# A gated mix of a diagonal SSM and an FFN on one core: three of B's seven slots are turned by DMA instead of TensorE, and the gates and C's scalings move in the order

## The chip, the cores and the metric

One core of a Trainium2 chip. The metric is device time in microseconds of one execution; the kernel before has a median of 138.81 us in 3 runs (138.67 to 138.88). The engines named are TensorE (PE, matrix products; PEld is its weight load), VectorE (DVE), ScalarE (ACT), GpSimd (POOL) and SyncE (SP), which here issues most of the DMAs. Each engine works through its own instructions in order; semaphores join them.

## The reference

For x of 2048 tokens by 448 features in bf16:

```python
g = sigmoid((x * gate_w).sum(-1, keepdims=True))
Lam_bar = exp(dt * Lam);  B_bar = ((Lam_bar - 1) / Lam)[:, None] * Bmat      # complex, 448 states
h[t] = Lam_bar * h[t-1] + B_bar @ x[t]
a = 2 * real(h @ Cmat.T) + x * Dskip
b = silu(x @ w1) @ w2                                                        # w1 448x1792, w2 1792x448
out = g * a + (1 - g) * b
```

## The kernel before, in words

**Stretches and slots.** The tokens are cut into four stretches of 512 (`tc` 0 to 3). The 448 complex states lie in seven slots of 128 partitions: slots 0 to 2 are the real parts of states 0 to 383, slots 4 to 6 their imaginary parts, and slot 3 holds the last 64 states, real parts in the lower half and imaginary parts in the upper. The recurrence is made real by turning each state by its own angle (tables `COS` and `SIN`), so that what is left is a decaying scan with one real factor per state.

**Work on TensorE, which is written out by hand.** For a stretch, `F(tc)` is fourteen tiles of silu(x w1), each 128 columns of w1 by 512 tokens, and `B(tc)` seven tiles of Bu, one for each slot. `x_products` takes tiles in pairs that share two PSUM banks; a pair is 14 matmuls of 64 rows, 8 in its first half and 6 in its second, and the first half of the next pair stands before the second half of the last one. `G` (line 837) is the second FFN product for 128 tokens, `C` (line 858) the readout for 128 tokens. The order is F(0) tiles 0 to 7 (`NHF`), B(0), the rest of F(0), B(1), F(1) with most of B(2), G for tokens of stretches 0 and 1, the rest of B(2) within F(2), B(3), F(3), C for stretches 0 and 1, G and C for stretch 2, G and C for stretch 3.

**Around it.** A product needs B with the feature on the partitions, so B must be transposed. Two ways exist: `rows_B` loads rows into `Bnat` (which lies in UG2), `b_transposes` (lines 666 to 676) turns them with 64x64 transposes on TensorE, and DVE and ACT copy the result from PSUM into `BT`; or `turn_B` issues a transposing DMA (line 452) straight into `BT`. Before, the real parts and slot 3 (slots 0 to 3) take the first way in two groups of two slots (`BPE`), 16 transposes a group, and the imaginary parts (slots 4 to 6) the second. `evict` takes pairs out of PSUM: silu on ACT for F (line 696), DVE for B of stretch 0 (703), ACT for later B (705). `lanes(tc)` is the recurrence of a stretch on DVE: products with the tables (767), seven scans (799), products back (767), with POOL casting each scan to bf16 by DMA (417), ACT doing this for the last stretch (809). `gates(tc)` computes g and x Dskip times g: two DVE products `xg` and `xd` (767) and eleven ACT steps (899 to 906). `readout_weights` scales C: two ACT copies (884, 885) and two DVE operations (887) for each of four slots of `ct`. `ffn2` ends in a DMA on POOL that adds into xnat (845). The readout is evicted by DVE (868) except for token blocks 8 to 11 (ACT, 863).

**Who sets the order of the other engines.** A planner (`Plan.order`) places every operation of ACT, DVE, POOL and SP in time from a cost of each, a priority (`prio`, lower goes first) and an earliest time (`at`), and what comes out is the fixed order of each engine. `GPR` are the priorities of the gates of the four stretches, `CTAT` is the earliest planned time of C's ACT copies, `LORD` the order of the loads on SP after the first ones, and `W1CUTS` the columns at which w1's load is cut. `MB`, `MP`, `GAT` say where parts of B(2) and the gates stand.

Of the kernel before, what the change touches and what calls it, by code (L numbers as in the profile page):

```python
# [28 lines left out]
XT1 = "da"  # L29
XDMA = (1, 2, 3)  # L30
XAFT = ["PO1"]
LORD = "Br BI w1 x1 g n1 w2 x2 C n2 n3".split()
BPE = ((0,2),(2,4))
TRATE = 2
MERGE = True
NHF = 8
MB = 6
MP = 3
GAT = 10
W1CUTS = [0, 256, 512, 1024, 1792]  # L40
L2AT = 1
UDVE = (0, 1, 2, 3, 4, 5, 6)
OUTA = (8, 9, 10, 11)
PRMF = (1, 0)
PRMP = 9.7
CPP = 20.5
CTAT = 59.0
GPR = (14, 20.3, 21.5, 19)
CASTB = (360000, 360000, 360000)
XCOL = [0, 128, 256, 320]  # L50

# [254 lines left out]
def bass_gated_mix__ssm_conv_s5__dense_activation_silu__prompt_kernel(nc, A_x, A_Lambda_re, A_Lambda_im, A_B_re, A_B_im, A_C_re, A_C_im,  # L306
               A_log_dt, A_Dskip, B_x, B_w1, B_w2, gate_w, out):
    with ExitStack() as ctx:
# [66 lines left out]
        g = sb("g", [128, NTB], F32)  # L375
# [5 lines left out]
        def sem():  # L381
            _s[0] += 1
            return E(nc.semaphore(name=f"d{_s[0]}"))
# [30 lines left out]
        def load(q, dst, src, name, nbytes, prio=None, after=()):  # L414
            nl[0] += 1
            prio = nl[0] if prio is None else prio
            P.add(q, lambda e: e.dma_start(dst, src), list(after), name.split(), 0.6 if q == "pool" else 0.5 if nbytes > 2000 else 0.35, prio, sem(), nbytes, tag="ld " + name)  # L417

        w1cuts = W1CUTS

# [21 lines left out]
        Bnat = UG[2][:, :, 0:D_MOD]  # L442
# [22 lines left out]
        def turn_B(a, r0, r1, to, slots):  # L465

            for c, n in ((0, 3), (3, 1)):
                names = [f"BT{s}T{c}_{to}" for s in slots]
                for s, m in zip(slots, names):
                    btn[s] = (btn[s] if s == 3 or c else []) + [m]  # L470
                turn(BT[:, c:c + n, to:to + r1 - r0], a[r0:r1, XCOL[c]:XCOL[c] + 128 * n], " ".join(names), (r1 - r0) * 256 * n, 0.7 + 0.0042 * n * (r1 - r0) / 4 * 1.0)

        def rows_B(a, r0, s0, s1, p0):
            if s1 - s0 > 1:
                load("sp", Bnat[:, s0:s1, :], a[r0:r0 + 128 * (s1 - s0), :].rearrange("(b p) d -> p b d", p=128), " ".join(f"U2_{s}" for s in range(s0, s1)), 128 * (s1 - s0) * 896)
            else:
                load("sp", Bnat[p0:p0 + 64, s0, :], a[r0:r0 + 64, :], f"U2_{s0}" + "i" * (p0 == 64), 64 * 896)

        def rows_g():
# [7 lines left out]
            "w4": lambda: [load_w1("sp", 4, r, r + 2) for r in (0, 2)],  # L487
            "Br": lambda: (rows_B(A_B_re, 0, 0, 3, 0), rows_B(A_B_re, 384, 3, 4, 0), rows_B(A_B_im, 384, 3, 4, 64)),
            "Bi": lambda: rows_B(A_B_im, 0, 4, 7, 0),
            "B2": lambda: rows_B(A_B_re, 0, 0, 2, 0),  # L490
            "BR": lambda: turn_B(A_B_re, 0, 448, 0, (0, 1, 2, 3)),
            "BH": lambda: turn_B(A_B_re, 256, 448, 256, (2, 3)),
# [6 lines left out]
        }  # L499
        for k in LORD:  # L500
            do[k]()
# [208 lines left out]
        def x_products(tiles, fill={}, wait=()):  # L710

            part = (list(zip([(i, 64) for i in (0, 1, 2, 3)], [(i, 0) for i in (0, 1, 3, 2)])),
                    list(zip([(i, 0) for i in (0, 1, 2)], [(i, 64) for i in (0, 1, 3)])))
            pairs = [tiles[t:t + 2] for t in range(0, len(tiles), 2)]
            toks = [Ps(2) for _ in pairs]

            def steps(k, h, a, z):
                def body(pe):
                    for n, cut in list(enumerate(part[h]))[a:z]:
                        for b, ((i, p0), tile) in enumerate(zip(cut, pairs[k])):
                            tc = tile[1]
                            r = pe.matmul(bk(toks[k], b), weights(tile, p0, p0 + 64, i), xT[p0:p0 + 64, tc, i, :],  # L726
                                          start=(h == 0 and n == 0), stop=(h == 1 and n == 2))
                    return r
                reads = [n for cut in part[h][a:z] for (i, _), tile in zip(cut, pairs[k])
                         for n in xn_of[tile[1]][i] + (w1n(tile[2], i) if tile[0] == "F" else btn[tile[2]])]  # L730
                return PE(body, list(dict.fromkeys(reads)), [toks[k]], (z - a) * PE_MM[512], f"{pairs[k][0][0]}{pairs[k][0][1]}")

            def half(k, h):
                if h == 0 and pairs[k][0] == ("F", 0, 0):
                    def zero(pe):
                        for n in range(NFILL):
                            for b, p in enumerate((slice(64, 128), slice(0, 64))):
                                r = pe.matmul(bk(toks[k], b)[:, 0:128], ones[p, 0:128], ones[p, 0:128], start=True, stop=True)
                        return r
                    PE(zero, [], [toks[k]], NFILL * 0.11, "fill")  # L740
                    steps(k, 0, 0, 2)
                    steps(k, 0, 2, 4)
                else:
                    steps(k, h, 0, len(part[h])).own = h == 1
                if h:
                    evict(pairs[k], toks[k])

            half(0, 0)
            for f in fill.get(-1, ()):
                f()  # L750
            for k in range(len(pairs)):
                order = [lambda: half(k, 1)] + [lambda: half(k + 1, 0)] * (k + 1 < len(pairs))
                for n, f in enumerate(order if k - 1 in wait else order[::-1]):
                    f()
                    for m in fill.get((k, n), ()):
                        m()
                for f in fill.get(k, ()):
                    f()

        def F(tc, a=0, b=NFB):  # L760
            return [("F", tc, k) for k in range(a, b)]

        def B(tc):
            return [("B", tc, k) for k in ((3, 0, 4, 1, 5, 2, 6) if tc else (0, 1, 2, 3, 4, 5, 6))]

        def tt(o, a, b, op, r, w, n, prio, tag=""):
            DVE(lambda e: e.tensor_tensor(o, a, b, op), r, w, dve_cost(n, 2), prio, tag)  # L767
# [152 lines left out]

        turn_b = [lambda a=a, z=z: b_transposes(a, z, "da") for a, z in BPE]
        NH = NHF
        K = NH // 2
        x_products(F(0, 0, NH) + B(0) + F(0, NH) + B(1),
                   {PRMF: [parameters], (K - 2, 0): turn_b[:1], K - 2: turn_b[1:2], K - 1: turn_b[2:], XT1K: xt(1, XT1) if 1 not in XDMA else [], 8: [lambda: lanes(0)] + [lambda: turn_x(3, XAFT)] * (3 in XDMA and bool(XAFT))}, [K - 2])
        gates(0)
        gates(1)
        lanes(1)
        if MERGE:
            b2 = B(2)[1:] + B(2)[:1]  # L930
            for f in cp(0, 1, 2, 3):
                f()
            x_products(F(1) + b2[:MB], {})
            gates(2)
            for f in G(0, 1, 2, 3, 4, 5, 6, 7):
                f()
            x_products(F(2, 0, MP) + b2[MB:] + F(2, MP) + B(3) + F(3), {L2AT: [lambda: lanes(2)], GAT: [lambda: gates(3)]})
# [51 lines left out]
```

## Time and profile before

| What | Value |
|---|---|
| median of 3 runs | 138.81 us (138.67 to 138.88) |
| profiled execution | 138.79 us, span 137.0 us |
| granted TensorE clock, mean | 0.997 |
| DVE busy | 118.9 us (87%) |
| ACT busy | 87.7 us (64%) |
| DMA moved | 16.83 MB, mean 123 GB/s |

The span is what lies between the first and the last instruction of the profiled execution. The rows of a timeline or of the chain read: start, duration, engine, line, operation, output <- input, tile shape, count. A row with x16 merges sixteen instructions and gives the time from the first start to the last end. A matmul's duration includes its way through the array, so that rows of consecutive matmuls overlap; the distance of the starts is what the engine spent. SPq is SP's queue, and a DMA's duration there is its issue, not its transfer; the time to landing is told apart.

### The profile page before, as it was taken

How to read it: one execution, taken by the hardware profiler on the slowest of the kernel's cores; microseconds unless marked ns; L12 is line 12 of the kernel's file. 1: busy time of each engine (PE TensorE's matmuls, PEld its weight loads, DVE VectorE, ACT ScalarE, POOL GpSimd, SP SyncE). 2: the span in 40 equal slices, each digit the busy share in tenths (PEclk: the TensorE clock that was granted, in tenths of full speed). 3: DMA queues.
4: the chain of work that ended last, by engine and by line, in shares of the span. 5: the costliest groups of instructions: out<-in, count | busy, mean ns of one | idle time of the engine just before them, and what ended most of it. 6: DMA issues, size and time to landing. Idle time of an engine off the chain costs nothing.

```text
span 137.0 us, 2606 instructions
## 1 busy us (share of the span) xinstructions
PE 133.3 (97%) x1017; PEld 66.9 (49%) x1017; DVE 118.9 (87%) x160; ACT 87.7 (64%) x156; POOL 42.0 (31%) x76
## 2 busy tenths in 40 slices
PE   7999999999999999999999999999999999999991
PEld 2544555555554555554444444445555555555561
DVE  0417999999999999999999999999999999997053
ACT  3239837999998993176699998699401129672200
POOL 7214030110246232685270031633000420366310
PEclk9999999999999999999999999999999999999998
DMA  4999789999877863299243010856222321249852
GB/s 145 320 237 260 158 223 366 229 131 194 268 128 120 151 110 53 41 145 167 41 72 51 0 38 5 113 81 106 77 86 89 67 43 24 34 66 123 151 135 68
DMA packets 27859, 16.83 MB, mean 123 GB/s; under 512 B 13507, under 2 KB 27718, under 8 KB 27846
## 3 DMA queue, kind: packets, MB, share of 16 engines
q1 hardware_dynamic: 20656, 10.33, 31.3%
q0 software_dynamic: 6640, 5.97, 29.6%
q10 hardware_dynamic: 550, 0.36, 0.8%
q8 instruction: 8, 0.13, 0.4%
q14 instruction: 5, 0.04, 0.1%
HBM read 5.97 MB, written 1.84 MB: 57 GB/s over the span
## 4 chain that ended last, share of the span: by engine, by line
PE 97%; DVE 1%; issue 0%
PE ps L726 47%; PE ps L837 31%; PE ps L858 16%; PE ps L523 2%; DVE xT L546 1%; PE ps L666 0%; PE ps L538 0%; DVE ot L868 0%; PE ps L524 0%; PE ps L598 0%
## 5 line engine op out<-in xcount | busy, mean ns | idle before, releaser
L726 PE MATMUL ps<-xT,w1s 64*128 64x512 bf16 x392 | 48.2, 380 | 0.2 <-DVE xT L546 0.2
L837 PE MATMUL ps<-w2s,aT 128*128 128x448 bf16 x224 | 42.9, 353 | 0.0
L696 ACT ACTIVATE aT<-ps 128x1024 bf16<-128x1024 f32 (+1 forms) x30 | 28.8, 963 | 9.6 <-PE ps L726 9.4
L726 PEld LDWEIGHTS ps<-xT,w1s 64*128 64x128 bf16 x392 | 21.4, 95 | 22.1 <-issue 0.9
L837 PEld LDWEIGHTS ps<-w2s,aT 128*128 128x128 bf16 x224 | 21.8, 98 | 20.7 <-issue 0.4
L726 PE MATMUL ps<-xT,BT 64*128 64x512 bf16 x196 | 26.1, 376 | 0.0
L799 DVE TENSOR_TENSOR_SCAN Gf<-rc,gin,H 128x512 f32<-128x512 f32 x21 | 25.3, 1267 | 0.1
L845 POOL DMA_DIRECT2D xnat<-fe x16 | 13.9, 868 | 36.2 <-ACT fe L843 36.2
L843 ACT ACTIVATE fe<-ps,g 128x448 bf16<-128x448 f32 x16 | 10.0, 628 | 22.3 <-PE ps L837 22.3
L417 POOL DMA_DIRECT2D UG<-Gf x27 | 15.0, 559 | 24.6 <-DVE Gf L799 24.3
L858 PE MATMUL ps<-CP,H 128*128 128x448 bf16 (+2 forms) x126 | 21.7, 332 | 0.0
L726 PEld LDWEIGHTS ps<-xT,BT 64*128 64x128 bf16 x196 | 11.7, 94 | 10.7 <-DVE Gf L586 0.4
L858 PEld LDWEIGHTS ps<-CP,H 128*128 128x128 bf16 x126 | 11.6, 98 | 10.0 <-DVE Gf L799 0.4
L767 DVE TENSOR_TENSOR H<-UG,COS 128x3584 bf16<-128x3584 bf16 (+2 forms) x9 | 16.1, 1810 | 0.0
L868 DVE SCALAR_TENSOR_TENSOR ot<-ps,g,xnat 128x448 bf16<-128x448 f32 (+2 forms) x14 | 8.2, 613 | 5.9 <-issue 4.6
L417 POOL DMA_DIRECT2D UG<-UG x8 | 4.8, 608 | 21.4 <-ACT UG L705 15.2
L705 ACT ACTIVATE UG<-ps 128x1024 bf16<-128x1024 f32 (+1 forms) x12 | 10.5, 918 | 0.5 <-PE ps L726 0.5
L906 ACT ACTIVATE xnat<-xnat,g 128x448 bf16<-128x448 bf16 x16 | 9.9, 661 | 0.2
L899 ACT ACTIVATE junk<-xg 128x448 bf16<-128x448 bf16 x16 | 9.2, 573 | 0.8 <-DVE xg L767 0.7
L767 DVE TENSOR_TENSOR PO<-UG,SIN 128x1536 bf16<-128x1536 bf16 (+1 forms) x8 | 8.6, 1084 | 0.0
L767 DVE TENSOR_TENSOR PI<-UG,SIN 128x1536 bf16<-128x1536 bf16 (+1 forms) x8 | 8.6, 1082 | 0.0
L767 DVE TENSOR_TENSOR H<-H,PI 128x3584 bf16<-128x3584 bf16 x4 | 8.1, 2020 | 0.1
(93 smaller groups left out, 97.9 us busy)
## 6 DMA issues: line engine op xcount, KB each, us to landing
UG<-Gf POOLq DMA_DIRECT2D x21, 128.0 KB, 2.3
xnat<-fe POOLq DMA_DIRECT2D x16, 112.0 KB, 2.6
w2s<-in_B_w_dram SPq DMA_DIRECT2D x1, 1568.0 KB, 10.2
xnat<-in_A_x_dram SPq DMA_DIRECT2D x3, 448.0 KB, 5.5
out_dram<-ot SPq DMA_DIRECT2D x11, 112.0 KB, 1.7
w1s<-in_B_w_dram SPq DMA_DIRECT2D x2, 384.0 KB, 4.7
w1s<-in_B_w_dram SPq DMA_DIRECT2D x2, 256.0 KB, 4.2
UG<-UG POOLq DMA_DIRECT2D x8, 64.0 KB, 4.2
```

The lines of the kernel that those rows point to most:

```text
L417: P.add(q, lambda e: e.dma_start(dst, src), list(after), name.split(), 0.6 if q == "pool" else 0.5 if nbytes > 2000 else 0.35, prio, sem() ...
L696: ACT(lambda e, src=src, dst=dst: e.activation(dst, src(), AF.Silu), [tk, "tbl"], [f"aT{tc % 2}_{m}" for m in names], act_cost(512 * n), 2 ...
L705: ACT(lambda e, src=src, dst=dst: e.activation(dst, src(), AF.Copy), [tk], after, act_cost(512 * n), 5, "U")
L726: r = pe.matmul(bk(toks[k], b), weights(tile, p0, p0 + 64, i), xT[p0:p0 + 64, tc, i, :], start=(h == 0 and n == 0), stop=(h == 1 and n == 2))
L767: DVE(lambda e: e.tensor_tensor(o, a, b, op), r, w, dve_cost(n, 2), prio, tag)
L799: DVE(lambda e, s=s, b=b, init=init: e.tensor_tensor_scan(Gf[:, s, :], rc[:, b:b + 1].to_broadcast([128, CH]), A[:, s, :], init, ALU.mult, ...
L837: r = pe.matmul(bk(tk)[:, 0:D_MOD], aT[tc % 2][:, fb, o:o + 128], w2s[:, fb, :], start=(fb == 0), stop=(fb == NFB - 1))
L843: ACT(lambda e: e.activation(f[:, :], bk(tk)[:, 0:D_MOD], AF.Copy, scale=g1[:, tb:tb + 1]), [tk, f"g1_{tc}"], [fn], act_cost(448, 1), 7, "fe")
L845: P.add("pool", lambda e: e.dma_start(Tb[:, tb, :], f[:, :], accum_op=ALU.add), [fn, f"Tb{tb}"], [f"Tb{tb}"], 0.94, 2, sem(), 250000, tag= ...
L858: r = pe.matmul(bk(tk)[:, 0:b - a], H[tc % 3][:, s, o:o + 128], CP[:, s, a:b], start=(s == 0), stop=(s == NSLOT - 1))
L899: ACT(lambda e, tb=tb, b=b: e.activation(junk[:, :], xg[:, b, :], AF.Copy, accum_out=zl[:, tb:tb + 1]), ["xg"], ["junk", f"zl{tc}"], act_c ...
L906: ACT(lambda e, tb=tb: e.activation(Tb[:, tb, :], xnat[:, tb, :], AF.Copy, scale=g[:, tb:tb + 1]), [f"xd{tc}", f"g_{tc}"], [f"Tb{tb}"], ac ...
```

## The change

B's real rows 0 to 383 (slots 0 to 2) are no longer loaded as rows and turned on TensorE; they come by two transposing DMAs, ahead of those of the imaginary part. Slot 3 alone is still loaded as rows (64 and 64) and turned on TensorE, 8 transposes instead of 32. w1's last 768 columns are loaded in two pieces of 384 (1024 to 1407 ahead of B's transposes, 1408 to 1791 behind them). Ten FFN tiles instead of eight stand ahead of the first Bu. The gates of stretch 2 are entered ahead of `lanes(1)`, with a new priority, those of stretch 3 get another one, and C's ACT copies may start at 46 of the planner's time instead of 59.

```diff
-LORD = "Br BI w1 x1 g n1 w2 x2 C n2 n3".split()
-BPE = ((0,2),(2,4))
+LORD = "Bs w3 BQ BI w4 x1 g n1 w2 x2 C n2 n3".split()
+BPE = ((3,4),)
-NHF = 8
+NHF = 10
+B0ORD = (0, 1, 2, 3, 4, 5, 6)
+GEARLY = (2,)
+GMID = ()
-W1CUTS = [0, 256, 512, 1024, 1792]
+W1CUTS = [0,256,512,1024,1408,1792]
-CTAT = 59.0
-GPR = (14, 20.3, 21.5, 19)
+CTAT = 46.0
+GPR = (14, 20.3, 20.4, 21.4)
...
+            "Bs": lambda: (rows_B(A_B_re, 384, 3, 4, 0), rows_B(A_B_im, 384, 3, 4, 64)),
+            "BQ": lambda: turn_B(A_B_re, 0, 384, 0, (0, 1, 2)),
...
         gates(0)
         gates(1)
+        for tc in GEARLY:
+            gates(tc)
         lanes(1)
...
             x_products(F(1) + b2[:MB], {})
-            gates(2)
+            for tc in GMID:
+                gates(tc)
...
```

The loads behind the names of `LORD` that stay: `w3` and `w4` are the upper and the lower rows of one piece of w1 each, `BI` turns the imaginary part into slots 4 to 6, `x1` and `x2` turn the second and third stretch of x, `g` loads the gate's and Dskip's rows, `n1` to `n3` load x's rows.

More of the change, by code (lines that the diff above doesn't have):

```diff
@@ L489, in bass_gated_mix__ssm_conv_s5__dense_activation_silu__prompt_kernel @@
             "Bi": lambda: rows_B(A_B_im, 0, 4, 7, 0),
+            "Bq": lambda: (load("sp", Bnat[:, 2, :], A_B_re[256:384, :], "U2_2", 128 * 896), rows_B(A_B_re, 384, 3, 4, 0), rows_B(A_B_im, 384, 3, 4, 64)),
+            "B0": lambda: turn_B(A_B_re, 0, 256, 0, (0, 1)),
+            "Bs": lambda: (rows_B(A_B_re, 384, 3, 4, 0), rows_B(A_B_im, 384, 3, 4, 64)),
+            "BQ": lambda: turn_B(A_B_re, 0, 384, 0, (0, 1, 2)),
             "B2": lambda: rows_B(A_B_re, 0, 0, 2, 0),
@@ L763, in B @@
         def B(tc):
-            return [("B", tc, k) for k in ((3, 0, 4, 1, 5, 2, 6) if tc else (0, 1, 2, 3, 4, 5, 6))]
+            return [("B", tc, k) for k in ((3, 0, 4, 1, 5, 2, 6) if tc else B0ORD)]
         def tt(o, a, b, op, r, w, n, prio, tag=""):
@@ L933, in bass_gated_mix__ssm_conv_s5__dense_activation_silu__prompt_kernel @@
             x_products(F(1) + b2[:MB], {})
-            gates(2)
+            for tc in GMID:
+                gates(tc)
             for f in G(0, 1, 2, 3, 4, 5, 6, 7):
                 f()
-            x_products(F(2, 0, MP) + b2[MB:] + F(2, MP) + B(3) + F(3), {L2AT: [lambda: lanes(2)], GAT: [lambda: gates(3)]})
+            x_products(F(2, 0, MP) + b2[MB:] + F(2, MP) + B(3) + F(3), {L2AT: [lambda: lanes(2)], GAT: [lambda: gates(3)] * (3 not in GEARLY + GMID)})
         else:
```

## The prediction

> **What bounds the kernel now.** I read the page's busy shares first, then the chain that ended last, then that chain in order of time.
>
> ```profile
> span 137.0 us, 2606 instructions
> PE 133.3 (97%) x1017; PEld 66.9 (49%) x1017; DVE 118.9 (87%) x160; ACT 87.7 (64%) x156; POOL 42.0 (31%) x76
> PE 97%; DVE 1%; issue 0%
> ```
>
> ```profile
> 5.17 4.06 PE ps L726 x30
> ...
> 11.03 0.23 PE ps L666 x16
> 11.26 0.65 PE ps L726 x6
> 11.91 0.23 PE ps L666 x16
> 12.14 30.99 PE ps L726 x286
> ...
> 91.73 10.70 PE ps L858 x56
> ...
> 128.91 5.34 PE ps L858 x42
> ```
>
> From 5.17 us to the last readout the chain is TensorE and nothing else: no DMA, no eviction ends a wait that TensorE feels. So an edit can gain only what it takes out of TensorE's own stream, and it loses whatever new wait it puts into that stream. The two L666 pieces are the transposes of B, the only TensorE work that the change touches. The run of 286 takes 30.99 us, 0.108 us for each product, so there is no hidden wait inside it to win either. The profiled execution took 138.79 us, 1.79 more than its span, and lies 0.02 under the median of 138.81; what I take off the span I take off both.
>
> **Part 1: transposes taken out.** The start times on TensorE:
>
> ```profile
> 9.34 1.69 PE L726 MATMUL ps<-xT,w1s 64*128 64x512 bf16 x14
> 10.86 0.40 PE L666 MATMUL ps<-ident,UG 64*128 64x64 bf16 x16
> 11.10 0.81 PE L726 MATMUL ps<-xT,w1s 64*128 64x512 bf16 x6
> 11.74 0.40 PE L666 MATMUL ps<-ident,UG 64*128 64x64 bf16 x16
> 11.98 0.81 PE L726 MATMUL ps<-xT,w1s 64*128 64x512 bf16 x6
> 12.62 4.38 PE L726 MATMUL ps<-xT,BT 64*128 64x512 bf16 x37
> ```
>
> Sixteen transposes hold the engine from 10.86 to 11.10 and from 11.74 to 11.98, 0.24 us each time, 15 ns for one; the 14 products before them go at 1.52/14 = 0.1086 us, the same rate as everywhere, so the switch costs nothing more. Before: 32 transposes, four slots. After: 8, slot 3 alone. 24 x 15 ns = **-0.36 us**. The number of products is unchanged; ten FFN tiles ahead instead of eight only reorders them. This is the whole gain that the trace offers.
>
> With it the new TensorE schedule follows by counting products from 9.34. The eighth and ninth FFN tiles (first to need columns from 1024 of w1) start after 20 products: 9.34 + 2.17 = 11.51. The 8 transposes stand at 12.38. The first Bu, which needs all of slots 0 to 2, starts after 40 products and 0.12: 13.80. Slots 4 to 6 follow after 22 more, 16.19; w1's columns from 1408 after 50 more, 19.23; xT of the second stretch after 64 more, 20.75.
>
> **Part 2: what now comes by DMA, and when.** SP's queue before:
>
> ```profile
> 3.80 1.07 SPq L417 DMA_DIRECT2D UG<-in_A_B_re_dram  x2
> ...
> 5.54 1.65 SPq L452 DMA_TRANSPOSE BT<-in_A_B_im_dram  x1
> 7.23 1.24 SPq L452 DMA_TRANSPOSE BT<-in_A_B_im_dram  x1
> 8.52 1.09 SPq L417 DMA_DIRECT2D w1s<-in_B_w_dram  x2
> 9.65 4.81 SPq L452 DMA_TRANSPOSE xT<-in_A_x_dram  x2
> 14.51 0.58 SPq L417 DMA_DIRECT2D gwb<-in_gate_w_dram  x1
> ...
> 16.64 9.62 SPq L452 DMA_TRANSPOSE xT<-in_A_x_dram  x2
> ```
>
> Time from issue to landing, one issue each: B_im's three columns and its fourth; w1's last 768 columns, upper and lower rows; x's second stretch; x's third, which queues behind w2 and is the longest of all.
>
> ```profile
> BT<-in_A_B_im_dram SPq DMA_TRANSPOSE x1, 4.7
> BT<-in_A_B_im_dram SPq DMA_TRANSPOSE x1, 3.3
> w1s<-in_B_w_dram SPq DMA_DIRECT2D x1, 384.0 KB, 3.8
> w1s<-in_B_w_dram SPq DMA_DIRECT2D x1, 384.0 KB, 5.7
> xT<-in_A_x_dram SPq DMA_TRANSPOSE x1, 6.4
> xT<-in_A_x_dram SPq DMA_TRANSPOSE x1, 11.0
> ```
>
> The change drops the 384-row load (half of the 1.07), adds two w1 loads ahead of the transposes (about 0.55 each by the 8.52 row) and two transposes (1.69 and 1.29 from start to next start by B_im's rows, the same shape). New issues: slot 3's rows 3.80 and 4.35; w1 1024 to 1407 at 4.98 and 5.53; B_re's transposes 6.08 and 7.77; B_im's 9.06 and 10.75; w1's rest 12.04 and 12.60; x's second stretch 13.17 and about 15.5 (half of 4.81 on); everything from gwb on 3.5 us later.
>
> Each against its need:
> - w1 1024 to 1407 lands at 5.53 + 3.8 to 5.7 = 9.3 to 11.2, needed 11.51. The bytes before it are nearly those before B's rows today, so I take the short end. Free, with 0.3 to 2.2 us of cover.
> - B_re lands at 6.08 + 4.7 = 10.8 and 7.77 + 3.3 = 11.1, needed 13.80: 2.7 us of cover. By the 6.4 row it would be 12.5, still early. By the 11.0 row it would be 17.1 and cost 3.3 us; that row stands behind the whole of w2, which is not yet issued here, so I go by B_im's rows, the same shape at nearly the same place.
> - B_im: 13.8 and 14.1 against 16.19. w1's rest: at most 12.60 + 5.7 = 18.3 against 19.23. xT: at most 13.17 + 6.4 = 19.6, its second piece 15.5 + 3.3 to 4.7 = 18.8 to 20.2, against 20.75: 0.5 us of cover at the worst, and more if it no longer queues behind 768 KB of w1. Free, all three.
> - x's third stretch: 16.64 + 3.5 + 11.0 = 31.1, its second piece about 2 later. It feeds the six Bu tiles (42 products, 4.6 us) that end the run at 43.13 (12.14 + 30.99), so it is needed past 38. w2, C and the other stretches have as much or more.
>
> B_re's turn on the DMA is where the skill speaks against the change. The Trainium skill, VectorE: DVE Perf Modes, section "The three transpose paths", gives 1309 ns for a 128x128 turn on the DMA crossbar against 390 on TensorE, and its rules advise TensorE. As an estimate from that page, B_re's twelve blocks in a row would take 15.7 us, land near 21.8, stop TensorE for 8 us and give 146.4. The trace disagrees on both: B_im's twelve blocks landed within 5.0 us of the first issue (7.23 + 3.3 - 5.54), and a block costs TensorE 2 x 15 ns here.
>
> **Part 3: evictions and the vector queues.**
>
> ```profile
> 12.39 0.41 DVE L674 COPY BT<-ps 128x512 bf16<-128x512 bf16 x1
> ...
> 18.39 1.21 DVE L703 CAST UG<-ps 128x1024 bf16<-128x1024 f32 x1
> ...
> 20.89 0.68 DVE L589 TENSOR_TENSOR Gf<-Gf 128x512 f32<-128x512 f32 x1
> ```
>
> DVE and ACT each copy two transposed groups out now (0.41 on DVE) and one of half the size after. That saves each some 0.5 us off the chain: nothing. Bu's evictions (1.21 for a pair) come 1.2 us later, as the first Bu does. A pair's PSUM is asked for again 28 products, 3.04 us, after the pair is complete. Eviction leaves 1.8 of that, and a parameter step that got in front of it (0.68 at most) leaves 1.1: free.
>
> ```profile
> 55.35 7.16 DVE L799 TENSOR_TENSOR_SCAN Gf<-rc,gin,H 128x512 f32<-128x512 f32 x6
> 62.43 4.35 DVE L887 SCALAR_TENSOR_TENSOR CP<-CP,sc1s,ct 128x448 bf16<-128x448 bf16 x7
> ...
> 69.56 1.09 DVE L767 TENSOR_TENSOR xg<-xnat,gwb 128x1792 bf16<-128x1792 bf16 x1
> ```
>
> The third stretch's gates (two DVE products of 1.09, eleven short ACT steps, no DMA) and seven of C's eight scalings (4.35/7 = 0.62 each, each behind one of ACT's copies, due at 46 instead of 59) now stand ahead of the second stretch's scans: 2 x 1.09 + 7 x 0.62 = 6.5 us. So these scans start near 62 instead of 55.35 and end near 71 (seven at 1.19 and the eighth scaling). POOL's queue has the same turn: seven of the FFN's accumulating DMAs now stand ahead of that stretch's casts instead of four, and the casts wait for the seventh FFN block, also near 63. Nobody on the chain needs the product before the fifth readout, 91.73 + 4 x 10.70/8 = 97. After the scans DVE no longer has the gates to do, so it is back on its old schedule when stretch three's scans begin; a wait for an ACT copy in between would cost it tenths. Cost nothing.
>
> ```profile
> 93.89 0.94 DVE L767 TENSOR_TENSOR PI<-UG,SIN 128x1536 bf16<-128x1536 bf16 x1
> 94.74 0.68 DVE L868 SCALAR_TENSOR_TENSOR ot<-ps,g,xnat 128x448 bf16<-128x448 f32 x1
> ...
> 111.38 8.34 DVE L799 TENSOR_TENSOR_SCAN Gf<-rc,gin,H 128x512 f32<-128x512 f32 x7
> ...
> 123.62 2.09 DVE L767 TENSOR_TENSOR H<-H,PO 128x2048 bf16<-128x2048 bf16 x2
> 130.34 0.68 DVE L868 SCALAR_TENSOR_TENSOR ot<-ps,g,xnat 128x448 bf16<-128x448 f32 x1 [4.63 <-issue]
> ```
>
> The end is where order matters. The changed order puts the first readout's eviction before the last two scans of stretch three and before the 1536-product of the 93.89 row. Before, DVE took 111.38 - 94.74 = 16.64 from that eviction to the last stretch's scans. After, the same piece holds two scans more (8.34/7 = 1.19 each) and that product (0.85 from 93.89 to 94.74): 19.87. It can't begin before the first readout is done: 91.73 - 0.36 + 10.70/8 = 92.71, and DVE, with that work taken out ahead of it, arrives near 91.5 and idles about 1.2 us. So the last scans begin at 112.6 instead of 111.38, and H for the last readouts ends at 112.6 + (125.71 - 111.38) = 126.9 instead of 125.71 (123.62 + 2.09). TensorE asks for it at 128.91 - 0.36 = 128.55. Cover falls from 3.2 to 1.6 us; cost nothing.
>
> **Sum.** 138.79 - 0.36 + 0 = 138.43, against the median 138.81 - 0.36 = **138.45**. A tenth of a microsecond either way is what the three runs differ by.
>
> **Rivals.**
> - *A short new wait eats the gain.* w1's piece, xT or a PSUM pair comes 0.1 to 0.6 us late. For it: covers of 0.3, 0.5 and 1.1 us at the long bounds. Against: those bounds belong to transfers behind twice the bytes. Time 138.5 to 139.0.
> - *B_re's turn is late (slower).* TensorE stops at the first Bu. It decides once the first piece takes over 7.7 us from issue or the second over 6.0. Speaking for it: the 11.0 row, 3.3 us of wait, 138.45 + 3.3 = 141.75; against: 4.7, 3.3 and 6.4. The skill page quoted above is this case at its far end.
> - *The last H is late (slower).* DVE reaches the first readout's eviction after 94.3 rather than 91.5, for instance held up by C's ACT copies; from there each microsecond is one on the end. 2.8 us of delay are needed; with 3.8 the time is 139.5. Against: DVE is there with idle time, so smaller delays vanish.
>
> **How the numbers follow.** Forecast 0.64, of which 0.56 beat the bound of 0.2% (0.28 us, about what a measurement of this kernel can tell from no change, so below 138.53) and 0.08 miss it by scatter. Short wait 0.16: a wait of 0.08 to 0.64 us leaves the time within the bound, 0.12, and 0.04 is slower. B_re late 0.08, last H late 0.10, both slower. A gain beyond 0.5 us, from some wait that I did not see, 0.02. So faster 0.58, same 0.20, slower 0.22. The forecast's own range is 138.3 to 138.6; to hold 8 in 10 I reach over the short waits: 138.25 to 139.2.
>
> **What would show it.** In the chain after: one L666-like piece of 8 transposes, about 0.12 us, near 12.4, then no break up to the last readout; the first Bu at 13.8; DVE idle once before the first eviction near 92.7 and its last wait down from 4.63 to about 3. Wrong if a DMA (B's transpose, w1, xT) or a DVE or ACT release appears as an idle end of TensorE, or if the readout of the last four blocks starts after a DVE product.

## The result and the profile after

| Compared | kernel before | changed kernel | ratio, 95% interval |
|---|---|---|---|
| first comparison, 12 runs each | 138.68 us (138.01 to 138.88) | 137.99 us (137.61 to 138.29) | 0.9961 [0.9947, 0.9975] |
| the same two again, 30 and 12 runs | 138.61 us (138.15 to 139.89) | 138.64 us (138.04 to 139.35) | 1.0002 [0.9973, 1.003] |
| both with TensorE held until 9.93 us (h1, h2 below), 12 runs each | 139.54 us (139.53 to 139.56) | 139.06 us (139.05 to 139.24) | 0.9966; by the extremes 0.9963 to 0.9979 |

The forecast was 138.45 us, in a range of 138.25 to 139.2, from a gain of 0.36. The first comparison gave 137.99, outside the range on the fast side. The third row is what the change is worth: 0.48 us. The first two rows differ from it, one in either direction; the experiments below put that down to the start of the program, ahead of all that the change touches. Medians count all runs of a kernel, and the ratios leave out those that ran more than 1.5% above its fastest.

The page of the changed kernel, and its chain in order of time (start, duration, what, count):

```profile
span 136.2 us, 2554 instructions
PE 132.4 (97%) x993; PEld 63.9 (47%) x993; DVE 118.5 (87%) x159; ACT 88.1 (65%) x155; POOL 42.0 (31%) x76
```

```profile
2.26 3.90 DMA w1s<-in_B_w_dram
6.16 0.14 issue
6.30 2.63 PE ps L733 x22
8.93 0.18 PE ps L605 x4
9.11 3.13 PE ps L733 x28
12.23 0.12 PE ps L673 x8
12.35 30.00 PE ps L733 x278
42.35 21.29 PE ps L844 x112
...
90.95 10.70 PE ps L865 x56
...
128.13 5.35 PE ps L865 x42
```

The profiled execution took 138.00 us. Lines are those of before plus 7 (726 is now 733, 837 is 844, 858 is 865). As foreseen there is one piece of transposes, 0.12 us near 12.2, and from 9.11 on nothing but TensorE. What was not foreseen stands in the run of products behind it: 278 products in 30.00 us are 0.1079 each, the 286 of before took 0.1084.

It helps to cut the span in two at the products that stand right behind the four small products of the parameters (9.11 here; in the chain of before the row is `9.41 1.62 PE ps L726 x14`). I call that moment the start. From the start to the first second-FFN product (42.35 here, 43.13 before) is the fixed part: 33.24 us here, 33.72 before. What follows is the same in both kernels.

| profiled execution | start | fixed part | span |
|---|---|---|---|
| before | 9.41 | 33.72 | 137.0 |
| changed | 9.11 | 33.24 | 136.2 |
| before, again | 9.61 | 33.72 | 137.2 |
| changed, again | 10.37 | 33.25 | 137.5 |

The fixed part repeats to 0.01 us; the start wanders by more than a microsecond. In these four executions the time less the start is 129.38 and 129.37 us for the kernel before, 128.89 and 128.90 for the changed one: what the fixed part does not account for, the start does. A median of 12 runs is a median over starts.

### The profile page after: what moved, and what is told of

Its sections match the earlier page's. It is cut to its first block, busy times and chain, and to the rows that moved or that the text cites. A ratio compares the mean times of both kernels' runs of the same rounds, so it can differ in the third digit from the quotient of the medians.

```text
span 136.2 us, 2554 instructions
## 1 busy us (share of the span) xinstructions
PE 132.4 (97%) x993; PEld 63.9 (47%) x993; DVE 118.5 (87%) x159; ACT 88.1 (65%) x155; POOL 42.0 (31%) x76
## 4 chain that ended last, share of the span: by engine, by line
PE 93%; DMA 3%; SPq 1%; issue 0%; DVE 0%
PE ps L733 46%; PE ps L844 31%; PE ps L865 16%; DMA w1s<-in_B_w_dram 3%; SPq L420 1%; DVE ot L875 0%; PE ps L605 0%; PE ps L673 0%
## 5 line engine op out<-in xcount | busy, mean ns | idle before, releaser
L733 PE MATMUL ps<-xT,w1s 64*128 64x512 bf16 x392 | 47.5, 376 | 0.3 <-DMA w1s<-in_B_w_dram 0.3
L733 PEld LDWEIGHTS ps<-xT,w1s 64*128 64x128 bf16 x392 | 20.0, 94 | 23.5 <-DMA w1s<-in_B_w_dram 0.7
L852 POOL DMA_DIRECT2D xnat<-fe x16 | 13.8, 861 | 35.6 <-ACT fe L850 34.1
L865 PEld LDWEIGHTS ps<-CP,H 128*128 128x128 bf16 x126 | 11.6, 98 | 10.0 <-DVE Gf L806 0.4
L733 PEld LDWEIGHTS ps<-xT,BT 64*128 64x128 bf16 x196 | 10.8, 94 | 11.5
## 6 DMA issues: line engine op xcount, KB each, us to landing
w2s<-in_B_w_dram SPq DMA_DIRECT2D x1, 1568.0 KB, 11.2
```

The costliest lines, as they stand in the source:

```text
L852: P.add("pool", lambda e: e.dma_start(Tb[:, tb, :], f[:, :], accum_op=ALU.add), [fn, f"Tb{tb}"], [f"Tb{tb}"], 0.94, 2, sem(), 250000, tag= ...
L865: r = pe.matmul(bk(tk)[:, 0:b - a], H[tc % 3][:, s, o:o + 128], CP[:, s, a:b], start=(s == 0), stop=(s == NSLOT - 1))
```

## The experiments

**The transposes alone, put back.** In the changed kernel each of the eight transposes is done four times, three of them for nothing, which makes 32 as before.

```diff
-                            r = pe.transpose(bk(tk, h).bitcast(BF16)[:, o:o + 64], Bnat[...], ident[p, p])
+                            for k in range(4):
+                                r = pe.transpose(bk(tk, h).bitcast(BF16)[:, 256 * k + o:256 * k + o + 64], Bnat[...], ident[p, p])
```

> The changed kernel, with each of slot 3's 8 transposes done four times over (the three copies go to PSUM columns that nobody reads), so TensorE again does 32 transposes while everything else stays. Theory A (the price of the transposes is 15 ns each, and the gain beyond it is a wait of the old kernel at its second pair of Bu): 0.36 us more than the changed kernel, so 0.49 - 0.36 = 0.13 us less than the kernel before plus what the start scatters: ratio to before about 0.999; on TensorE the time from the start of the first product after the parameters to the first G is 33.24 + 0.36 = 33.60. Theory B (most of the gain comes from the start, where fewer bytes are in flight behind w1's first pieces): the start stays early, and the ratio stays near 0.997.

Measured: 138.56 us, ratio 0.9973 [0.9942, 1.0004], profiled 138.63. The fixed part is 33.61, so the 24 transposes are worth 0.37 us, 15 ns each, as the forecast had it; the ratio's interval is too wide to tell that from nothing. But before has 33.72: 0.11 to 0.12 us of the gain is something else.

**The other tenth: ACT's copy of the second transposed group.** The kernel before, TensorE's weight loads and ACT near the first Bu (start, duration, ..., in brackets the idle time before):

```profile
13.57 2.93 PEld L726 LDWEIGHTS ps<-xT,BT 64*128 64x128 bf16 x29 [0.42 <-DVE Gf L586]
```

```profile
11.95 1.02 ACT L696 ACTIVATE aT<-ps 128x1024 bf16<-128x1024 f32 x1
12.87 0.59 ACT L676 ACTIVATE BT<-ps 128x512 bf16<-128x512 bf16 x1
```

The second group's half that ACT copies stands behind a silu and ends at 13.46; the weight loads stop for 0.42 and go on at 13.57. The row names a step of DVE as the releaser; ACT's copy is what ends last before the weight loads go on, and the experiment decides between the two. In the experiment DVE copies both halves of the second group, in the kernel before:

```diff
-        turn_b = [lambda a=a, z=z: b_transposes(a, z, "da") for a, z in BPE]
+        turn_b = [lambda a=a, z=z: b_transposes(a, z, "dd" if a else "da") for a, z in BPE]
```

> The kernel before, with both copies of the second transposed group on DVE instead of one on ACT, where it stands behind a silu. Theory A: the break of 0.12 us on TensorE at the second pair of Bu (starts 0.334 apart instead of 0.216) is gone, the time from the first product after the parameters to the first G falls from 33.73 to 33.61, the whole by 0.12 us (ratio 0.999). Theory B, or the break comes from something else: the break stays, 33.73.

Measured: 138.40 us, ratio 0.9975 [0.9945, 1.0006], profiled 138.65. The weight loads and the chain of this kernel:

```profile
12.40 3.77 PEld L726 LDWEIGHTS ps<-xT,BT 64*128 64x128 bf16 x36
```

```profile
12.13 30.86 PE ps L726 x286
```

The break is gone and the same 286 products take 30.86 instead of 30.99 us. That is the hidden wait, 0.13 us; the changed kernel loses it too, because its only transposed group is slot 3, whose Bu is the fourth.

**The transposing DMA alone, and eight tiles ahead.** The first leaves w1 uncut, eight tiles ahead of the first Bu, gates and C as before; the second is the changed kernel with eight tiles.

```diff
-LORD = "Br BI w1 x1 g n1 w2 x2 C n2 n3".split()
-BPE = ((0,2),(2,4))
+LORD = "Bs BQ BI w1 x1 g n1 w2 x2 C n2 n3".split()
+BPE = ((3,4),)
```

```diff
-NHF = 10
+NHF = 8
```

> The kernel before with one part of the change alone: slots 0 to 2 come by transposing DMA, slot 3 alone is turned on TensorE; eight FFN tiles ahead, w1's last 768 columns in one piece, gates and C as before. Theory A: the first Bu is asked for near 12.3 and B's real part lands near 10.8, so no wait there: the same 33.24 on TensorE, ratio 0.996 as the whole change. Rival C (the ten tiles and the cut of w1 are needed as cover): TensorE waits at the first Bu for the transposing DMA or at the ninth FFN tile for w1, 0.3 us or more, ratio 0.999 or above.

> The changed kernel with eight FFN tiles ahead of the first Bu instead of ten; w1's cut, the loads' order, the gates and C stay. The first Bu is asked for near 12.3, B's real part lands near 10.8 in the profiles so far. Theory A: no difference in a profile, 33.24 on TensorE. Theory E (the two tiles more are cover that is needed in the executions whose DMAs are late; the kernel with the turn alone measured 139.12, with 0.49 us less on TensorE in its one profile): the profile may show 33.24, but the median is some 0.3 to 0.8 us above the changed kernel's.

Measured: 139.12 us, ratio 1.0014 [0.9982, 1.0046], profiled 138.44; and 138.82 us, ratio 1.0006 [0.9981, 1.0031], profiled 138.84. By the medians neither gains. By the profiles both have the whole gain: the fixed part is 33.24 in either, from starts at 9.45 and 9.94. So neither w1's cut nor the ten tiles earns anything that the profile can see.

**B's rows loaded as before, unread.** The changed kernel with 336 KB more ahead of the rest of SP's queue.

```diff
-LORD = "Bs w3 BQ BI w4 x1 g n1 w2 x2 C n2 n3".split()
+LORD = "Br w3 BQ BI w4 x1 g n1 w2 x2 C n2 n3".split()
```

> The changed kernel with the load of B's 384 real rows put back in its old place on SP's queue; nobody reads it. Theory B (the start gains since 336 KB behind w1's pieces are gone): the start is later by 0.2 to 0.5, the time 0.2 to 0.5 us above the changed kernel's. Theory A: everything behind it on SP moves by 0.5 us within its cover, 33.24, no difference beyond 0.1%.

Measured: 138.34 us, ratio 1.0001 [0.9977, 1.0025], profiled 138.19. TensorE in it:

```profile
15.94 1.88 PE L733 MATMUL ps<-xT,BT 64*128 64x512 bf16 x15 [0.22 <-DMA BT<-in_A_B_im_dram]
```

With the queue 0.5 us later and an early start (8.8) TensorE waits for B's imaginary part. The covers of the loads are real but thin; in the profiles of the changed kernel itself nothing is late. With these bytes back the start is no later in this profile and the median no higher (138.34 against 138.64 for the changed kernel in the same comparison), so nothing here says that they delay the start.

**Both kernels again.** No edit.

> The kernel before, unchanged, timed against itself: what two equal kernels differ by in such a comparison, and a second profile of its start. All theories: ratio 1.000 within 0.001. Theory A: 33.73 again from the first product after the parameters to the first G, and the break of 0.12 at the second pair of Bu is there again; the first product after the parameters, 9.34 in the first profile, moves by tenths. Theory B: it is again at 9.3 or later, not near 9.0.

> The changed kernel, unchanged, beside the kernel before once more, since the kernel before differed from itself by 0.24% in the last comparison. Theory A: 33.24 on TensorE from the first product after the parameters to the first G, and a ratio of about 0.996. Theory D (what is left beyond 0.49 us is scatter of the start, w1's first pieces landing early or late): the start (first product after the parameters) is anywhere between 9.0 and 9.6.

Measured: 138.56 us, ratio 0.9976 [0.9945, 1.0008], for the kernel before, and the second row of the first table for the changed one. TensorE in the profile of the changed kernel, this time:

```profile
4.96 1.09 PE L733 MATMUL ps<-xT,w1s 64*128 64x512 bf16 x8
7.64 2.55 PE L733 MATMUL ps<-xT,w1s 64*128 64x512 bf16 x22 [1.59 <-DMA w1s<-in_B_w_dram]
```

The same piece of w1, issued at 2.25, landed at 7.50 instead of 6.16 (chain: `2.25 5.25 DMA w1s<-in_B_w_dram`), and the whole program ended 1.26 us later. This piece is issued ahead of everything that the change touches.

**Starting when the first pieces of w1 are there.** 21 more warm-up products in either kernel, used by nobody.

```diff
-            for _ in range(NWARM):
+            for _ in range(NWARM + 21):
```

> The kernel before with 21 more warm-up products ahead of the first FFN product (their result is used by nobody, and the order of all engines' other work stays as it is), so that the first product starts only when the first pieces of w1 have landed. Theory A (the change takes 0.49 us out of the part between TensorE's first product and the first G, 0.36 by transposes and 0.12 by a hidden wait for ACT's copy of the second transposed group; the rest of the differences between runs is the start, which the landing of w1's first pieces sets): every time becomes longer by what the start becomes later, about 4 us, so 142.5 to 143.5, and the scatter shrinks below 0.3 us. All loads are earlier against TensorE, ACT's copy too, so the 0.12 wait may go: fixed part 33.60 to 33.73. Rival D (the scatter lies elsewhere, in the end or in the middle): the times scatter by over 1 us as before.

> The changed kernel with the same 21 more warm-up products. Theory A: the same later start as in the kernel before with them, fixed part 33.24, so 0.36 to 0.48 us less than that kernel in the same call, ratio of the two 0.9967 to 0.9975, with little scatter on either. Rival D (the gain of the change comes from an earlier start, w1's cut or the shorter queue ahead of it): with the start made the same the two are within 0.2 us. Rival with covers: the loads of the changed kernel being earlier against TensorE, nothing can be late here; if it gains more than 0.5 us, the changed kernel loses something in its own form that this one does not.

Measured: 142.74 us (142.22 to 143.70, 6 runs; ratio 1.0305 [1.027, 1.034]) and 142.99 us (142.24 to 143.34, 6 runs; 1.0313 [1.0283, 1.0343]). The theory that w1's landing alone makes the scatter falls: in the two profiles no product waits for w1, and the runs still differ by 1.1 to 1.5 us. The first rows of TensorE in the two, and the same rows of the kernel before:

```profile
0.76 7.33 PE L523 MATMUL ps<-const-bfloat16-1.0 128*128 128x512 bf16 x27 [0.76 <-PEq L974]
9.22 3.41 PE L726 MATMUL ps<-xT,w1s 64*128 64x512 bf16 x30
```

```profile
0.76 8.35 PE L530 MATMUL ps<-const-bfloat16-1.0 128*128 128x512 bf16 x27 [0.76 <-PEq L984]
10.24 3.41 PE L733 MATMUL ps<-xT,w1s 64*128 64x512 bf16 x30
```

```profile
0.76 2.72 PE L523 MATMUL ps<-const-bfloat16-1.0 128*128 128x512 bf16 x6 [0.76 <-PEq L974]
3.27 0.42 PE L524 MATMUL ps<-const-bfloat16-1.0 128*128 128x256 bf16 x1
```

The same 27 products end 1.02 us apart. Six of them took 2.51 us from the first start to that of the next row, 0.42 each; at the rate of the later products (two of 0.108) one takes 0.216. So TensorE begins at half its rate and goes over to the full one at a moment that differs from run to run: with 0.42 and 0.216, 6.5 slow products in the one and 11.6 in the other, or full rate from 3.5 and from 5.6 us. Each microsecond of delay costs half a microsecond. In the profiles of the kernels without more warm-up it came at 4.9 us or earlier in some and near 6.7 us in others. The clock row shows nothing of this change, it has nines throughout in both profiles; the products' own times show it. The rest of the page agrees: the fixed parts are 33.72 and 33.24 here too.

The Trainium skill, TensorE: Matmul & The Clock Gate, Part 1, has this: the array starts at half its clock, is let go after about 3.4 us of activity seen by a window that runs freely, and the number of slow products therefore differs from run to run. That the moment differs from run to run agrees with the 3.5 and 5.6 us here. The sizes do not all agree: from the first product at 0.76 the change came after 2.7 us in one run, earlier than 3.4, and after 4.8 in the other, and the two lie 2.1 us apart where the page gives 0.5 either way.

**Holding TensorE until a fixed time.** POOL does idle iotas behind its own first work, and TensorE's four small products of the parameters wait for them. What happened before no longer reaches the end.

```diff
+NGATE = 20
...
+        for _ in range(NGATE):
+            POOL(lambda e: e.iota(gt[:, :], pattern=[[1, 200]], base=0, channel_multiplier=0), ["hpi", "SG"], ["gt"], 0.01, 2)
...
-            PE(prm_t, prmn + ["prm4", "ident"], [tkp], 0.5, "prmT")
+            PE(prm_t, prmn + ["prm4", "ident", "gt"], [tkp], 0.5, "prmT")
```

It was put into the kernel before, the changed one, the one with the transposing DMA alone, and the one with the transposes put back.

> The kernel before with 20 idle iotas of 200 columns on POOL behind its own first operations, and TensorE's four small products of the parameters waiting for them (about 9.5 to 10.3 us), so that all that lies before, the landing of w1's first pieces and the moment at which TensorE's products go from 0.427 a pair to 0.216 (3.6 to 6.7 us in the profiles so far), no longer reaches the end. Theory S (all scatter between runs of one kernel arises before the parameters' products): the runs lie within 0.3 us of each other. Theory M (part of the scatter arises later, in waits of TensorE for loads that one profile need not show): they scatter by a microsecond as before. Time: start + 33.73 + 93.93 + 1.8, 139.0 to 139.9.

> The changed kernel with the same gate. Theory S with a fixed part shorter by 0.49 us: the runs lie within 0.3 us of each other and 0.45 to 0.5 us below those of the kernel before with the gate. Theory M: the changed kernel scatters by more than the kernel before, or gains less than 0.3 us, because some of its runs wait for B's or w1's transfers after the first Bu.

> Only the transposing DMA in place of 24 transposes (eight tiles ahead, w1 uncut, gates and C as before), with the same gate. Theory S: as the changed kernel with the gate, within 0.1 us. Theory M: this one had 139.12 without the gate in spite of a fixed part of 33.24; if it waits for transfers in some runs, it scatters here and its median lies 0.3 us or more above that of the changed kernel.

> The changed kernel with 24 transposes put back at the place of the eight (each of the eight done four times, three of them for nothing), with the same gate. By 24 x 15 ns it is 0.36 us above the changed kernel with the gate, and 0.12 us below the kernel before with the gate, if ACT's copy of the second transposed group was worth the remaining 0.12. If the transposes were worth more or less than the profile's 15 ns, the difference shows it.

Twenty iotas took longer than meant; TensorE went on at 11.74 us, after 3 us of idling, and in part of the runs it had fallen back to half rate (granted clock 0.976 to 0.988 instead of 1.0). The medians (142.02, 141.70, 142.54 and 142.78 us) mix the two kinds. The runs with a clock of 0.999 or 1.0:

| kernel with the gate | runs at full clock | us |
|---|---|---|
| before (g1) | 3 of 6 | 141.34, 141.34, 141.35 |
| changed (g2) | 3 of 6 | 140.87, 140.96, 140.98 |
| transposing DMA alone (g4) | 2 of 6 | 140.86, 140.97 |
| changed, transposes put back (g5) | 2 of 6 | 141.23, 141.24 |

The row of TensorE and the clock row of the transposing DMA alone, whose profile shows the fallback:

```profile
11.74 0.23 PE L609 MATMUL ps<-ident,prm 3*128 3x3 bf16 x4 [3.01 <-POOL gt L527]
11.91 3.17 PE L737 MATMUL ps<-xT,w1s 64*128 64x512 bf16 x14
```

```profile
PEclk9996899999999999999999999999999999999999
```

14 products take 3.17 us where they took 1.69 before, and the clock row has a dent in its fourth and fifth slice. In the runs at full clock the scatter is 0.11 us or less, the transposing DMA alone equals the whole change within that, and the transposes put back cost 0.25 to 0.37.

The last two runs have 15 iotas, in the kernel before and in the changed one.

```diff
-NGATE = 20
+NGATE = 15
```

> The kernel before with the gate of 15 iotas on POOL instead of 20; an iota and its wait took 0.36 us (4.40 to 11.59 for 20), so the parameters' products start at 4.40 + 15 x 0.36 + 0.15 = 9.95, 1.8 us earlier: 141.34 - 1.8 = 139.55, within 0.1 us in all runs whose first pieces of w1 are in time, and without half rate behind the gate, since TensorE idles for 1.5 us at most.

> The changed kernel with the gate of 15 iotas. If the forecast's sum was right (transposes alone), it lies 0.36 us below the kernel before with this gate; if the hidden wait for ACT's copy comes on top, 0.48 us: 139.07. Nearer to 0.36 than to 0.48 would leave the 0.12 of the profile unproven in time.

Measured: 139.54 us (139.53 to 139.56) and 139.06 us (139.05 to 139.24), against 138.50 for the kernel before without a gate (ratios 1.0068 [1.0048, 1.0089] and 1.003 [1.001, 1.005]). The chains of the two:

```profile
9.93 0.23 PE ps L602 x4
10.16 1.62 PE ps L730 x14
...
12.89 31.00 PE ps L730 x286
43.89 21.29 PE ps L841 x112
```

```profile
9.93 0.23 PE ps L609 x4
10.16 3.13 PE ps L737 x28
13.29 0.12 PE ps L677 x8
13.40 30.00 PE ps L737 x278
43.41 21.29 PE ps L848 x112
```

Both start at 10.16; 43.89 and 43.41 are 0.48 apart, and so are the times. Twelve runs of a kernel that otherwise scatters by more than a microsecond lie within 0.03, those of the changed kernel within 0.19. So all but 0.2 us of the scatter arises ahead of the parameters' products, and the change is worth 0.48 us, not 0.36.

**The gates and C's scalings.** Four kernels: the changed one with both moves undone; the changed one with C's copies early and the gates where they were; the kernel before with both moves alone; and the transposing DMA alone (above), which has neither move.

```diff
-GEARLY = (2,)
-GMID = ()
+GEARLY = ()
+GMID = (2,)
-CTAT = 46.0
-GPR = (14, 20.3, 20.4, 21.4)
+CTAT = 59.0
+GPR = (14, 20.3, 21.5, 19)
```

The second kernel has the same diff without the two CTAT lines; the third has the moves of the change on the loads of before.

> The changed kernel with the gates' places and priorities and C's due time as before. All theories so far: nothing of it is on TensorE's chain, 33.24 and the same time as the changed kernel within 0.2%. Rival: DVE or ACT get late somewhere behind the first G, and the time from the first G to the last readout (90.96 in both profiles) is longer.

> The changed kernel with the gates of stretches two and three entered where and with the priorities they had before; C's ACT copies stay at 46. Both moves undone cost 2.0 us against the changed kernel's profile (0.14 of start aside): DVE waited 2.8 us for the casts of stretch one, then ACT's copies of C waited for DVE, and TensorE waited 1.85 us near 67.4 for PSUM. Theory F1 (C's early scalings are the work that fills DVE's wait for the casts): time as the changed kernel, span = start + 33.24 + 93.93 with no new wait of TensorE. Theory F2 (the gates' two products of 1.09 us are what fills it and keeps ACT's order): 1 to 2 us slower, span about 1.3 to 1.9 longer than start + 33.24 + 93.93, with a wait of TensorE near 67 us.

> The kernel before with the gates' and C's move alone; loads, transposes, w1's cut and the eight tiles as before. Theory F (the move is worth nothing by itself, it is cover that the changed loads need): fixed part 33.73, TensorE without a new break after it, span = start + 33.73 + 93.93, ratio 1.000 within 0.003. Rival G (the move is worth something by itself, or costs it: DVE's or ACT's turn reaches TensorE): a break of 0.2 us or more after the first G, or a shorter time by the same.

Measured: 140.06 us (139.00 to 142.35 in 7 runs), ratio 1.0074 [1.0027, 1.0121]; 139.19 us, ratio 1.0035 [1.001, 1.006]; 138.61 us, ratio 1.001 [0.9981, 1.004]. The moves alone on the kernel before do nothing (fixed part 33.73, no new wait). Without them the changed loads lose: the changed kernel had 138.64 in the same comparison as the 140.06. What the moves seem to cover shows in the casts of the first stretch, POOL's DMAs near 40 us (size, then us from issue to landing); before, changed kernel, transposing DMA alone:

```profile
UG<-Gf POOLq DMA_DIRECT2D x2, 128.0 KB, 2.3
```

```profile
UG<-Gf POOLq DMA_DIRECT2D x1, 128.0 KB, 5.3
```

```profile
UG<-Gf POOLq DMA_DIRECT2D x1, 128.0 KB, 2.8
```

In the changed kernel SP's queue reaches its last big loads of x (448 KB each) at 35.83, in the run with the DMA alone at 33.96; the casts begin near 36, while these loads are under way. With the DMA alone the first cast takes 4.8 us and the last of 128 KB 2.3, so I put the delay down to the loads; no run changes the loads of x alone. DVE waits for a cast in the changed kernel, and longer in the profile with the moves undone:

```profile
45.49 0.96 DVE L774 TENSOR_TENSOR PO<-UG,SIN 128x1536 bf16<-128x1536 bf16 x1 [1.90 <-DMA UG<-Gf]
```

```profile
46.56 0.96 DVE L774 TENSOR_TENSOR PO<-UG,SIN 128x1536 bf16<-128x1536 bf16 x1 [2.82 <-DMA UG<-Gf]
65.35 0.67 ACT L891 ACTIVATE ct<-CP,scc 128x448 f32<-128x448 bf16 x1 [3.89 <-DVE CP L894]
69.48 1.69 PE L733 MATMUL ps<-xT,w1s 64*128 64x512 bf16 x14 [1.69 <-ACT aT L703]
```

How long that wait is differs from execution to execution, since up to there the two have the same order: in the five profiles of the changed kernel and of its variants with both moves, from starts as they come, it is 0.87 to 2.18 us, and TensorE does not stop behind it; in the two without one or both moves it is 2.82 and 3.14; in the changed kernel held until 9.93 there is none. So no profile shows the moves against a wait as long as 2.82. With the moves undone, DVE's delay reaches ACT's copies of C, the silu behind them, and TensorE, which stops for 1.69 us. With C's copies alone early, in a profiled execution that was the slowest of its runs (140.64), it is the gate that bites: they push DVE's scans back, the gate's product comes behind the scans, and ACT's sum over it stands ahead of a silu:

```profile
72.54 0.58 ACT L906 ACTIVATE junk<-xg 128x448 bf16<-128x448 bf16 x1 [3.46 <-DVE xg L774]
```

```profile
74.18 1.90 PE L733 MATMUL ps<-xT,w1s 64*128 64x512 bf16 x15 [1.69 <-ACT aT L703]
```

So my two theories for the second kernel were both half right: C's move without that of the gates puts a wait of ACT in front of TensorE. The gates' move without C's was not run. How often the stop happens in the runs of the second kernel (137.96 to 140.64) one profile doesn't show. None of it is needed with the load order of the DMA alone, where DVE waits for no cast.

## Why the prediction was right or wrong

**The step that failed** in the mechanism is in the first part: "The run of 286 takes 30.99 us, 0.108 us for each product, so there is no hidden wait inside it to win either." There was one of 0.12 to 0.13 us, shown by the run that took it away (30.86 for the same 286 products): TensorE waited for ACT's copy of the second transposed group. The mean hid it: 0.13 us over 286 products is 0.0005 each, and the two rates agree to three digits. The chain doesn't break there: it shows the engine with its short stop as one piece. The stop was to be read from the weight loads' row with its 0.42 of idle time, and from ACT's copy behind a silu. In the third part the copies saved on ACT were put at "off the chain: nothing"; one of them was on it.

**The term that was right:** 24 transposes at 15 ns, 0.36. Measured 0.37 in the profile with them put back.

**The sum** was therefore -0.36 where h1 and h2 measured -0.48. From 138.81 that gives 138.33, inside the forecast's own range, so the hidden wait alone would not have put the time outside it. That the first comparison showed 137.99 needs 0.34 more: its kernel before had a median 0.13 lower than 138.81, and 0.21 is left for the starts. That split is worked out, not measured; that starts can do it, the second comparison shows, where the same two kernels came out equal. Its 138.64 lies inside the range, by luck of the same kind.

**"A tenth of a microsecond either way is what the three runs differ by"** was the other step that failed, and the one that put the first median outside the range: the three runs happened to agree. Runs of either kernel differ by 0.7 to 1.7 us within a comparison, medians of one and the same kernel by 0.65 (137.99 and 138.64), and the sum put this at nothing. A gain beyond 0.5 us was given a chance of 0.02, from an unseen wait; the wait was there, but with it the gain is 0.48, and the rest of the 0.69 in the first comparison is put down to the starts.

**The landings** held. The rows of SP's queue and the landing times of the changed kernel (one issue each: w1's columns from 1024, B's real part in two, its imaginary part, x's third stretch):

```profile
5.03 1.10 SPq L420 DMA_DIRECT2D w1s<-in_B_w_dram  x2
6.17 3.23 SPq L455 DMA_TRANSPOSE BT<-in_A_B_re_dram  x2
9.44 2.65 SPq L455 DMA_TRANSPOSE BT<-in_A_B_im_dram  x2
...
19.10 10.81 SPq L455 DMA_TRANSPOSE xT<-in_A_x_dram  x2
```

```profile
w1s<-in_B_w_dram SPq DMA_DIRECT2D x1, 192.0 KB, 4.0
BT<-in_A_B_re_dram SPq DMA_TRANSPOSE x1, 4.6
BT<-in_A_B_re_dram SPq DMA_TRANSPOSE x1, 3.6
BT<-in_A_B_im_dram SPq DMA_TRANSPOSE x1, 4.9
xT<-in_A_x_dram SPq DMA_TRANSPOSE x1, 14.5
```

w1's piece, both halves issued by 5.6, landed near 9.6 (said: 9.3 to 11.2). B's real part landed at 6.17 + 4.6 = 10.8 (said: 10.8), its second piece 3.6 after an issue near 8.2, so at 11.8 (said: 11.1); the first Bu started at 13.48. Its imaginary part landed at 9.44 + 4.9 = 14.3 (said: 13.8). The rival that B's turn is late did not come true, and neither did the estimate of 146.4 us, worked out with 1309 ns for each block in a row from the Trainium skill (VectorE: DVE Perf Modes, "The three transpose paths"): twelve blocks landed within 5.6 us of the first issue, and TensorE did not wait for them. x's third stretch took 14.5, longer than the bound of 11.0, and was still in time at 33.6. Of the rival of a short new wait nothing is in the changed kernel's profile; it appeared only where 336 KB were put back.

**The gates at "Cost nothing"** was right as a sum and wrong as a picture. I looked at the order of DVE and POOL and not at what the later loads do to the casts. DVE waits 1.90 us there that it did not wait before, and it does not idle for 1.2 us ahead of the readout's first eviction, as I had it.

**The end** came as worked out, two numbers a little earlier: last scans at 112.43 (said: 112.6), DVE's last wait down to 2.79 (said: about 3), H complete at 126.76 (said: 126.9).

```profile
112.43 8.34 DVE L806 TENSOR_TENSOR_SCAN Gf<-rc,gin,H 128x512 f32<-128x512 f32 x7
...
124.67 2.09 DVE L774 TENSOR_TENSOR H<-H,PO 128x2048 bf16<-128x2048 bf16 x2
129.55 0.68 DVE L875 SCALAR_TENSOR_TENSOR ot<-ps,g,xnat 128x448 bf16<-128x448 f32 x1 [2.79 <-issue]
```

TensorE asks for H at 128.13, so 1.4 us of the 3.2 are left (said: 1.6). The rival that the last H is late stayed away. That the numbers agree is partly luck: the delay by the cast took up the idle time that I had counted on, and DVE reached the first eviction at 92.58, just behind the first readout's end (90.95 + 10.70/8 = 92.29).

Open is why the runs with the transposing DMA alone had a median of 139.12: with the gate it equals the changed kernel, so by the runs here it was the start, but no trace of those runs shows it.

## What to carry to other kernels

Read a run of products on TensorE by the gaps between starts, not by its mean: a stop of a tenth disappears in a mean over hundreds, and the weight loads' row shows it. Before forecasting a few tenths, ask how far the program's start wanders; if it does, hold both kernels at a fixed time with idle work on a free engine, short enough that TensorE stays at its full rate, and differences of 0.1 us can be measured. Moves in the order of other engines that look like part of a gain may only pay for what the same change's loads do to them: try the loads without the moves, in more than one order of the loads.

## What the runs showed of the hardware that was not expected

- TensorE's first products run at half rate (0.42 us for 512 columns instead of 0.216), and the change to full rate came at 3.5 us in one run and 5.6 in another, behind the same first products of the two kernels.
- After 2.9 to 3.1 us of idling (four profiles) TensorE had fallen back in 14 of 24 runs, for 1.3 to 1.7 us of lost time at a mean granted clock of 0.988 and 2.6 to 3.1 at 0.976; two of the four profiled executions had fallen back (after 3.01 and 2.96 us), two had not (after 3.08 and 2.93). After 1.0 us of idling (15 iotas) it fell back in none of 24.
- The same DMA of w1, fourth in SP's queue, landed 3.90 us after its issue in one execution and 5.25 in another, and the program ended 1.26 us later.
- A cast of 128 KB by POOL's DMA landed after 2.3 us in the kernel before and after 5.3 in the changed one, where two loads of 448 KB were under way at the same time; in the second profile of the changed kernel such casts took 3.8 to 6.1 us.
